# GpSimd's word additions and lower-half subtractions issued as two column halves, in an attention and MLP-mixer kernel

## The chip, the cores and the metric

The kernel runs on one core of one Trainium2 chip. The metric is the device time of one execution in microseconds (us). Five engines work side by side, each on its own queue of instructions in the order in which the program emitted them: TensorE (PE; its weight loads are shown as PEld), VectorE (DVE), ScalarE (ACT), GpSimd (POOL) and SyncE (SP), which here issues all transfers. They wait for each other by semaphores.

## The reference

A linear attention over four batches, four heads, 1088 positions and 32 channels per head; then two mixers, over positions and over channels:

```python
a = einsum('rd,bhsd->bhsr', S1, x); b = einsum('rd,bhsd->bhsr', S2, x)      # r = 8
phi(x) = (a_i * b_j), 64 features
kv = phi(k)^T v;  z = sum of phi(k) over positions
x = (phi(q) kv) / (phi(q) z + 1e-6)          # to [4, 1088, 128]
h = relu(x^T w_tok1) w_tok2                  # 1088 -> 256 -> 1088
u = x + h^T
out = u + relu(u w_ch1) w_ch2                # 128 -> 1536 -> 128
```

All inputs and the output are float32. The weights reach the kernel as float64 words (a 64-bit integer view), and the device itself turns them into float32.

## The kernel before, in words

The work goes batch by batch. For each batch there are `keys` (K: project, square into features, sum against v), queries (Q), `mixing` (A: attention, then the product with w_tok1, a transposition, the product with w_tok2), and for 384-column spans of all batches `channel_mix` (U: 12 hidden chunks; per chunk a first product with w_ch1 on PE, a ReLU copy on ACT, its remainder on DVE, a second product with w_ch2 on PE). From batch 1 on the mixing, and everywhere the channel mix, keeps float32 accuracy with three products of a short format: each operand is a high half (`halves[..][:, 0]`) and a low half (`halves[..][:, 1]`), and the products are high x high, low x high, high x low. Batch 0's mixing uses the undivided weights (`whole`).

The weights come in 17 pieces: `w00` to `w04` of w_tok1 (four of 512 columns, one, `w04`, of 256), `w10` to `w15` of w_tok2 (four of 384, two of 320), `w20` to `w22` of w_ch1 and `w30` to `w32` of w_ch2 (512 each). Each piece goes through this chain (`convert`, lines 333 to 372, then `divide_weight`, lines 437 to 451):

- `.abs` (ACT, line 343) and `.low` (ACT, line 347): the magnitude of the upper word, and the scaled lower word.
- `.clamp` (DVE, line 350), `.shift` (DVE, line 354, into PSUM bank `ps_h`), `.merge` (DVE, line 357).
- `.add` (POOL, lines 361 and 363): the lower word is added; this gives the float32 weight.
- `.hi` (ACT, line 444): the copy to the short format, the high half.
- `.lo` (POOL or DVE, whichever the planner takes, line 447): the weight less its high half.

What sets the order is a planner in the kernel (`Plan.run`, lines 187 to 261). It is a list scheduler that runs while the program is built: each step has an estimated cost for each engine that may do it (`act`, `dve`, `either`, ...), a level (its longest remaining path, plus `BOOST`, plus an entry of `LEAD` in ns), and the buffers it takes. The planner walks its own clock, always takes a step that can start first, among those the one of highest level, and emits it at once. So costs and levels alone decide each engine's order, and also how many filler products (`fill`, line 319, into an unused bank, row L322 of the profile) are put where PE is expected to be idle. Steps marked `port=True` on DVE (`.clamp` among them) and all POOL steps are kept apart on the planner's clock by one shared variable, `port`. For `.lo`, DVE is charged 1300 ns (`PBIAS`) on top. `LEAD` has 62 entries.

A short-format product can't start before the `.lo` that it reads; `is_whole` and `is_split` (lines 433 and 451) hold the last step of a piece's `.add` and `.lo`, and the products of A (`.t`, line 794; `.w`, line 912) and U (`.f`, line 974; `.s`, line 978) name them.

Of the kernel before, what the change touches and what calls it, by code (L numbers as in the profile page):

```python
# [15 lines left out]
ALU = mybir.AluOpType  # L16
# [23 lines left out]
def _spans():  # L40
# [27 lines left out]
    "A0.u2": 900.0,  # L68
    "A0.ul00": 51100.0,
    "A0.w2": 9300.0,  # L70
    "A1.t0": -6100.0,
    "A1.x": 36300.0,
    "A2.n0": 110900.0,
    "A2.n2": 110000.0,
    "A2.uh05": -52300.0,
    "A2.w2": -16300.0,
    "A3.n0": 18000.0,
    "A3.us1": 38200.0,
    "K0.s18": 52100.0,
# [6 lines left out]
    "Q0.b01": 29200.0,  # L86
    "Q0.b11": -8100.0,
    "Q0.p0": 54300.0,
    "Q1.m10": -20100.0,
    "Q1.m11": -21200.0,  # L90
    "Q2.p": 10200.0,
    "U0.f": 780300.0,
    "U11.f": 1400.0,
    "U2.f": -4000.0,
    "U4.f": 1480700.0,
    "U7.f": -2900.0,
# [8 lines left out]
    "w04.lo": -148800.0,  # L105
    "w04.low": 12100.0,
    "w10.abs": 19800.0,
    "w11.abs": 27600.0,
# [38 lines left out]
def f32(ap):  # L147
    return ap.bitcast(F32)
# [119 lines left out]
def act_sb(n):  # L268
    return {"act": 100 + 0.834 * n}
# [10 lines left out]
def either(n):  # L280
    return {"dve": 69 + 1.042 * n, "pool": 141 + 2.15 * n}
# [3 lines left out]
def attn_mixer_kernel(ctx: ExitStack, tc: tile.TileContext, qT, kT, v1, s64, wt1, wt2, wc1, wc2, out):  # L285
    nc = tc.nc
    engines = {"dve": nc.vector, "pool": nc.gpsimd, "act": nc.scalar}
# [3 lines left out]
    pool = ctx.enter_context(tc.tile_pool(name="pool", bufs=1))  # L291
# [32 lines left out]
    def load(name, dst, src, nbytes, after=(), takes=(), uses=(), boost=0.0):  # L324
# [3 lines left out]
        op.bytes, op.rate = nbytes, 395.0  # L328
        return op

    def convert(name, raw, n, loaded, dst=None, keep=None):


        t = {}
        c_hold, tail_hold, ps_hold = keep or Hold("c"), Hold("tail"), Hold("ps_h")
        words = raw.bitcast(I32).rearrange("p (n t) -> p n t", t=2)
        low, high = words[:, :, 0], words[:, :, 1]

        def magnitude(_):
            t["c"] = const.tile([P, n], I32, name="s_c") if keep else new("c", [P, CONV], I32)[:, :n]
            nc.scalar.activation(f32(t["c"]), f32(high), AF.Abs)  # L343

        def rest(_):
            t["tail"] = new("tail", [P, CONV], I32)[:, :n]
            nc.scalar.activation(t["tail"], low.bitcast(U32), AF.Copy, scale=2.0 ** -29)  # L347

        def clamp(_):
            nc.vector.tensor_scalar(f32(t["c"]), f32(t["c"]), LEAST, MOST, op0=ALU.max, op1=ALU.min)  # L350

        def shift(_):
            t["ps"] = bank("ps_h").bitcast(I32)[:, :n]
            nc.vector.tensor_scalar(t["ps"], t["c"], 3, 0x3FFFFFFF, op0=ALU.logical_shift_left, op1=ALU.bitwise_and)  # L354

        def merge(_):
            nc.vector.scalar_tensor_tensor(t["c"], high, -(1 << 30), t["ps"], op0=ALU.bitwise_and, op1=ALU.bitwise_or)  # L357

        def add(e):
            if dst:  # L360
                engines[e].tensor_tensor(dst(), t["c"], t["tail"], op=ALU.add)  # L361
            else:
                engines[e].tensor_tensor(t["c"], t["c"], t["tail"], op=ALU.add)
# [73 lines left out]
    def divide_weight(w, i, after=()):  # L437
        n = pieces[w, i].shape[1]
        name = f"w{w}{i}"
        m, t, c_hold = converted[w, i]  # L440

        def high(e):
            halves[w, i] = const.tile([P, 2, n], F32R, name=f"halves{w}{i}", tag=f"weight{w}{i}")
            nc.scalar.copy(halves[w, i][:, 0], f32(whole[w, i] if w < 2 else t["c"]))

        def low(e):
            engines[e].tensor_tensor(halves[w, i][:, 1], f32(whole[w, i] if w < 2 else t["c"]), f32(halves[w, i][:, 0]), op=ALU.subtract)  # L447
# [262 lines left out]
    def mixing(b, kvz_done, qp_done, qp_hold, boost, free):  # L710
# [63 lines left out]
        for g in range(3):  # L774
            def first(_, g=g):
# [117 lines left out]
        for i, (c0, cn) in enumerate(CHUNKS):  # L893
# [3 lines left out]
            def second(_, i=i, c0=c0, cn=cn):  # L897
# [45 lines left out]
    def channel_mix(segs):  # L943

        o_holds, outs = {}, {}
        for i, e0, e1 in segs:
# [3 lines left out]
            for e in range(e0, e1):  # L950
# [20 lines left out]
                        nc.tensor.matmul(outs[i][:, :cn], lhsT=part(3, at[3][e][0], l, at[3][e][1] * P, P), rhs=r[:, :cn], start=(e == 0 and m == 0), stop=(e == NCH - 1 and m == 2))  # L971
# [6 lines left out]
                s = plan.add(n + ".s", {"pe": cost}, second, [m, is_split[3, at[3][e][0]]], [o_hold] if e == 0 else (), [hid] + ([o_hold] if e else []), 0.0, 0, 2 * cost, [chain["s"]])  # L978
                chain["s"] = s
                if e == NCH - 6:  # L980
                    first_out = s
            if e1 == NCH:
# [6 lines left out]
                def add(_, i=i, cn=cn):  # L989
                    nc.vector.tensor_tensor(outs["sb", i][:, :cn], outs["sb", i][:, :cn], outs[i][:, :cn], op=ALU.add)  # L990
# [87 lines left out]
```

## Time and profile before

| | |
|---|---|
| time, median of 3 runs | 224.47 us (223.86 to 225.18) |
| the profiled execution's own time | 224.15 us |
| its span, first to last instruction | 222.3 us (1.85 us lie around it) |
| PE busy | 215.3 us |
| DVE busy | 141.3 us |
| ACT busy | 118.4 us |
| POOL busy | 80.5 us |

A row of the timeline has the start, the duration, the engine, the line of the program, the operation, what it writes and reads with its size, and how many instructions follow each other (`x2`); in brackets stands the engine's idle time before it and who ended it. The duration of a row of several runs from the start of the first to the end of the last. The instructions of DVE and POOL overlap a little at their ends, so the distance from one start to the next is often shorter than the duration. A step's name (w03.clamp) follows from the order in which the planner emitted the steps of that engine; most can also be told by size and line.

### The profile page before, as it was taken

How to read it: one execution, taken by the hardware profiler on the slowest of the kernel's cores; microseconds unless marked ns; L12 is line 12 of the kernel's file. 1: busy time of each engine (PE TensorE's matmuls, PEld its weight loads, DVE VectorE, ACT ScalarE, POOL GpSimd, SP SyncE). 2: the span in 40 equal slices, each digit the busy share in tenths (PEclk: the TensorE clock that was granted, in tenths of full speed). 3: DMA queues.
4: the chain of work that ended last, by engine and by line, in shares of the span. 5: the costliest groups of instructions: out<-in, count | busy, mean ns of one | idle time of the engine just before them, and what ended most of it. 6: DMA issues, size and time to landing. Idle time of an engine off the chain costs nothing.

```text
span 222.3 us, 4915 instructions
## 1 busy us (share of the span) xinstructions
PE 215.3 (97%) x1904; PEld 203.4 (91%) x1904; DVE 141.3 (64%) x273; ACT 118.4 (53%) x284; POOL 80.5 (36%) x85
## 2 busy tenths in 40 slices
PE   7999799999999999999999999999999999999994
PEld 7787658989988999999999899999999999999993
DVE  1689997998868465755825355657445655656662
ACT  4398499987446144553524354445235554445551
POOL 2074676989999401660500410443102300000000
PEclk9999999999999999999999999999999999999999
DMA  6999972999302999500060248400340000100000
GB/s 196 408 405 410 408 316 58 207 169 192 149 3 74 260 233 195 200 28 0 33 208 12 61 110 172 184 0 3 125 125 0 8 30 0 37 3 35 0 32 24
DMA packets 11207, 28.42 MB, mean 128 GB/s; under 512 B 1456, under 2 KB 5552, under 8 KB 11184
## 3 DMA queue, kind: packets, MB, share of 16 engines
q1 hardware_dynamic: 11184, 28.11, 41.4%
q8 instruction: 15, 0.25, 0.5%
q14 instruction: 8, 0.07, 0.1%
HBM read 23.27 MB, written 4.83 MB: 126 GB/s over the span
## 4 chain that ended last, share of the span: by engine, by line
PE 83%; DVE 9%; DMA 4%; issue 1%; POOL 1%; ACT 0%; POOLq 0%
PE ps_o L971 30%; PE ps_h L958 30%; PE ps_a L788 4%; PE ps_a L908 4%; PE ps_a L726 4%; DMA v_sb<-v 4%; PE ps_o L322 3%; DVE c L357 2%; PE ps_a L521 2%; DVE ps_h L354 2%; PE ps_a L474 2%; DVE c L350 2%; DVE hl L965 1%; PE ps_a L608 1%; DVE k_p L504 1%
## 5 line engine op out<-in xcount | busy, mean ns | idle before, releaser
L965 DVE SCALAR_TENSOR_TENSOR hl<-ps_h,hh 128x384 fp32r<-128x384 f32 (+2 forms) x144 | 75.3, 533 | 57.7 <-ACT hh L962 51.9
L962 ACT ACTIVATE hh<-ps_h 128x384 fp32r<-128x384 f32 (+2 forms) x144 | 67.8, 477 | 60.0 <-PE ps_h L958 51.6
L958 PE MATMUL ps_h<-uh,halves 128*128 128x384 f32 (+2 forms) x288 | 89.0, 332 | 0.1
L971 PE MATMUL ps_o<-hh,halves 128*128 128x384 f32 (+2 forms) x288 | 71.6, 330 | 0.1
L958 PEld LDWEIGHTS ps_h<-uh,halves 128*128 128x128 f32 x288 | 53.4, 188 | 1.9 <-issue 0.9
L971 PEld LDWEIGHTS ps_o<-hh,halves 128*128 128x128 f32 x288 | 50.2, 188 | 0.9 <-POOL halves L447 0.6
L971 PE MATMUL ps_o<-hl,halves 128*128 128x384 f32 (+2 forms) x144 | 47.2, 328 | 0.0
L958 PE MATMUL ps_h<-ul,halves 128*128 128x384 f32 (+2 forms) x144 | 46.9, 326 | 0.0
L958 PEld LDWEIGHTS ps_h<-ul,halves 128*128 128x128 f32 x144 | 27.1, 188 | 0.1
L882 POOL TENSOR_TENSOR ul<-us,uh 128x64 fp32r<-128x64 f32 (+4 forms) x15 | 9.5, 657 | 48.6 <-ACT uh L879 48.6
L971 PEld LDWEIGHTS ps_o<-hl,halves 128*128 128x128 f32 x144 | 27.1, 188 | 0.0
L706 POOL TENSOR_TENSOR qp<-qp,br 128x544 f32<-128x544 f32 x12 | 16.3, 1376 | 9.8 <-DMA br<-rows 9.8
L754 POOL TENSOR_TENSOR xl<-x,xh 128x384 fp32r<-128x384 f32 x9 | 9.0, 1020 | 15.9 <-ACT den L734 15.1
L504 DVE TENSOR_TENSOR k_p<-ps_a,a_sb 128x1024 f32<-128x1024 f32 (+1 forms) x12 | 10.9, 950 | 5.5 <-ACT a_sb L484 5.5
L361 POOL TENSOR_TENSOR whole<-c,tail 128x512 int32<-128x512 int32 (+3 forms) x11 | 12.0, 1093 | 4.8 <-DVE c L357 4.0
L322 PE MATMUL ps_o<-ident 128*128 128x128 f32 x66 | 11.0, 326 | 1.4 <-POOL ident masks.py:199 1.4
L322 PEld LDWEIGHTS ps_o<-ident 128*128 128x128 f32 x66 | 10.2, 233 | 1.9 <-POOL ident masks.py:199 1.4
L447 POOL TENSOR_TENSOR halves<-whole,halves 128x512 fp32r<-128x512 f32 (+3 forms) x11 | 11.9, 1103 | 0.0
L343 ACT ACTIVATE c<-doubles 128x512 f32<-128x512 f32 (+3 forms) x17 | 10.6, 637 | 1.8 <-POOL whole L361 1.4
L350 DVE TENSOR_SCALAR c<-c 128x512 f32<-128x512 f32 (+3 forms) x17 | 11.3, 677 | 0.0
L347 ACT ACTIVATE tail<-doubles 128x512 int32<-128x512 uint32 (+3 forms) x17 | 10.4, 644 | 1.5 <-POOL whole L361 1.5
L726 PEld LDWEIGHTS ps_a<-kvz,qp 128*64 128x64 f32 x288 | 9.0, 137 | 1.8 <-issue 1.2
(76 smaller groups left out, 238.8 us busy)
## 6 DMA issues: line engine op xcount, KB each, us to landing
qp<-rows SPq DMA_DIRECT2D x6, 544.0 KB, 9.4
br<-rows SPq DMA_DIRECT2D x12, 272.0 KB
doubles<-wc SPq DMA_DIRECT2D x6, 512.0 KB
v_sb<-v SPq DMA_DIRECT2D x4, 594.0 KB, 13.0
k_sb<-kT SPq DMA_DIRECT2D x4, 576.0 KB, 10.2
q_sb<-qT SPq DMA_DIRECT2D x4, 544.0 KB, 9.9
doubles<-wt SPq DMA_DIRECT2D x4, 512.0 KB, 7.7
xm<-xb SPq DMA_DIRECT2D x3, 576.0 KB, 2.9
```

The lines of the kernel that those rows point to most:

```text
L322: nc.tensor.matmul(spare_ps[:, :P], lhsT=ident, rhs=ident, start=True, stop=True)
L343: nc.scalar.activation(f32(t["c"]), f32(high), AF.Abs)
L350: nc.vector.tensor_scalar(f32(t["c"]), f32(t["c"]), LEAST, MOST, op0=ALU.max, op1=ALU.min)
L361: engines[e].tensor_tensor(dst(), t["c"], t["tail"], op=ALU.add)
L447: engines[e].tensor_tensor(halves[w, i][:, 1], f32(whole[w, i] if w < 2 else t["c"]), f32(halves[w, i][:, 0]), op=ALU.subtract)
L504: engines["pool" if on_pool else "dve"].tensor_tensor(t["k_p"][:pn, t0 * H:t1 * H], a.unsqueeze(3).broadcast_to([pn, n, R, R]), t["sb", t0 ...
L706: engines[e].tensor_tensor(qp[:, p, cs], qp[:, p, cs], t["br"][:, p, cs], op=ALU.mult)
L726: nc.tensor.matmul(x_ps[c:c + 64, o:o + 2 * (D + 1)], lhsT=qp[:, p, s0 + c:s0 + c + 64], rhs=kvz_all[b % 2][:, p, :], start=True, stop=True,)
L958: nc.tensor.matmul(h_ps[:, :cn], lhsT=part(2, at[2][e][0], l, at[2][e][1] * P, P), rhs=r[:, :cn], start=(m == 0), stop=(m == 2))
L962: nc.scalar.activation(t["hh"][:, :cn], t["h"][:, :cn], AF.Relu)
L965: nc.vector.scalar_tensor_tensor(t["hl"][:, :cn], t["h"][:, :cn], 0.0, f32(t["hh"][:, :cn]), op0=ALU.max, op1=ALU.subtract)
L971: nc.tensor.matmul(outs[i][:, :cn], lhsT=part(3, at[3][e][0], l, at[3][e][1] * P, P), rhs=r[:, :cn], start=(e == 0 and m == 0), stop=(e == ...
```

## The change

`add` and `low` get a slice of columns, and `in_parts` makes two planner steps out of each, with half of the columns and their own cost: `.add0` and `.add1` for the 17 pieces (the small constant `s` keeps its one addition on DVE), `.lo0` and `.lo1` for each division. The two halves of one step have the same predecessors; what followed one step now follows both (`.hi` waits for both additions, the products wait for both subtractions). Operations, operands and results are the same; 34 instructions become 68.

Besides, `LEAD` is other: it has 112 entries. Those of the six steps that were split pass to their halves (two of these with other values), 45 steps have an entry that had none, six values are changed and one entry (`U2.f`) is gone. The diff shows the core of it.

```diff
-    "A1.t0": -6100.0,
-    "A1.x": 36300.0,
-    "A2.n0": 110900.0,
+    "A1.n0": 71100.0,
+    "A1.t0": -6600.0,
+    "A1.w2": -100.0,
+    "A1.x": 65800.0,
...
+    "K2.p": 274800.0,
...
+    "w00.add0": 15600.0,
     "w00.hi": -188600.0,
-    "w00.lo": -296700.0,
-    "w02.lo": -1516300.0,
-    "w03.lo": -12100.0,
-    "w03.merge": -5300.0,
+    "w00.lo0": -296700.0,
+    "w00.lo1": -296700.0,
+    "w01.lo0": -270400.0,
+    "w01.lo1": -346700.0,
+    "w02.hi": -570400.0,
+    "w02.lo0": -1516300.0,
+    "w02.lo1": -1516300.0,
+    "w02.shift": -109900.0,
...
+    "w03.merge": 12400.0,
...
+    "w04.shift": 94300.0,
...
+    "w14.abs": -252800.0,
...
+    "w30.low": -71100.0,
...
+    def in_parts(n, make):
+
+        half = (n + 1) // 2
+        return [make(i, slice(a, min(n, a + half))) for i, a in enumerate(range(0, n, half))]
...
-        def add(e):
-            if dst:
-                engines[e].tensor_tensor(dst(), t["c"], t["tail"], op=ALU.add)
-            else:
-                engines[e].tensor_tensor(t["c"], t["c"], t["tail"], op=ALU.add)
+        def add(e, cs=slice(0, n)):
+            if dst and "to" not in t:
+                t["to"] = dst()
+            engines[e].tensor_tensor(t.get("to", t["c"])[:, cs], t["c"][:, cs], t["tail"][:, cs], op=ALU.add)
...
-        ways = {"dve": 69 + 2.084 * n} if keep else {"pool": 141 + 2.15 * n}
-        m = plan.add(name + ".add", ways, add, [m, r], (), [c_hold, tail_hold], port=True)
+        if keep:
+            return plan.add(name + ".add", {"dve": 69 + 2.084 * n}, add, [m, r], (), [c_hold, tail_hold], port=True), t, c_hold
+
+        m = in_parts(n, lambda i, cs: plan.add(f"{name}.add{i}", {"pool": 141 + 2.15 * (cs.stop - cs.start)}, lambda e, cs=cs: add(e, cs), [m, r], (), [c_hold, tail_hold], port=True))
...
-        def low(e):
-            engines[e].tensor_tensor(halves[w, i][:, 1], f32(whole[w, i] if w < 2 else t["c"]), f32(halves[w, i][:, 0]), op=ALU.subtract)
+        def low(e, cs):
+            engines[e].tensor_tensor(halves[w, i][:, 1, cs], f32(whole[w, i] if w < 2 else t["c"])[:, cs], f32(halves[w, i][:, 0, cs]), op=ALU.subtract)
...
-        m = plan.add(name + ".hi", act_sb(n), high, [m], (), use, order=after)
-        is_split[w, i] = plan.add(name + ".lo", either(n), low, [m], (), use, port=True)
+        m = plan.add(name + ".hi", act_sb(n), high, m, (), use, order=after)
+        is_split[w, i] = in_parts(n, lambda k, cs: plan.add(f"{name}.lo{k}", either(cs.stop - cs.start), lambda e, cs=cs: low(e, cs), [m], (), use, port=True))
```

The four places that name `is_whole` and `is_split` take the lists in place of the single steps.

More of the change, by code (lines that the diff above doesn't have):

```diff
@@ L81 @@
     "K1.c0": 73400.0,
+    "K1.s": 136500.0,
+    "K2.c0": -27100.0,
+    "K2.c8": -48200.0,
+    "K2.p": 274800.0,
+    "K2.s": 57400.0,
+    "K2.v4": 151900.0,
+    "K2.v8": 2570300.0,
     "K3.p": 82600.0,
@@ L88 @@
     "Q0.p0": 54300.0,
+    "Q1.c0": -5100.0,
+    "Q1.m00": -20200.0,
     "Q1.m10": -20100.0,
@@ L92 @@
     "U0.f": 780300.0,
+    "U0.oh": 14700.0,
+    "U1.f": 2100.0,
+    "U10.f": 1500.0,
     "U11.f": 1400.0,
-    "U2.f": -4000.0,
+    "U3.f": 74000.0,
     "U4.f": 1480700.0,
-    "U7.f": -2900.0,
+    "U5.f": 535300.0,
+    "U6.f": 371600.0,
+    "U7.f": 40600.0,
+    "w00.add0": 15600.0,
     "w00.hi": -188600.0,
-    "w00.lo": -296700.0,
-    "w02.lo": -1516300.0,
-    "w03.lo": -12100.0,
-    "w03.merge": -5300.0,
+    "w00.lo0": -296700.0,
[6 more added lines that the diff above has]
+    "w02.shift": -109900.0,
+    "w03.hi": 2300.0,
+    "w03.lo0": -67100.0,
+    "w03.lo1": -12100.0,
+    "w03.merge": 12400.0,
     "w04.abs": 70300.0,
@@ L104 @@
     "w04.hi": 8600.0,
-    "w04.lo": -148800.0,
-    "w04.low": 12100.0,
+    "w04.lo0": -148800.0,
+    "w04.lo1": -148800.0,
+    "w04.low": 92400.0,
+    "w04.shift": 94300.0,
     "w10.abs": 19800.0,
+    "w10.hi": 55100.0,
     "w11.abs": 27600.0,
@@ L113 @@
     "w12.abs": -1200.0,
-    "w12.lo": 7000.0,
+    "w12.lo0": 7000.0,
+    "w12.lo1": 7000.0,
     "w12.low": 159700.0,
     "w13.clamp": -55300.0,
+    "w13.lo0": 9300.0,
+    "w13.lo1": -171700.0,
+    "w13.low": -11300.0,
+    "w14.abs": -252800.0,
     "w14.low": -113600.0,
     "w15.clamp": 34000.0,
+    "w15.lo1": -11700.0,
     "w15.low": -82500.0,
-    "w20.add": -18200.0,
+    "w15.shift": 107300.0,
+    "w20.add0": -18200.0,
+    "w20.add1": -18200.0,
+    "w20.clamp": -10300.0,
     "w20.low": 45700.0,
     "w21.abs": -10800.0,
+    "w21.hi": -385300.0,
+    "w21.low": -82000.0,
+    "w22.abs": 600.0,
+    "w22.add1": -7900.0,
     "w22.low": 6300.0,
     "w30.abs": -6400.0,
+    "w30.low": -71100.0,
     "w30.merge": 75500.0,
     "w31.abs": -10200.0,
+    "w31.lo1": -25300.0,
     "w32.low": -196200.0,
@@ L793, in mixing @@
             last = plan.add(
-                f"{n}.t{g}", {"pe": 9 * 120.0 if b else 3 * 430.0}, first, [split[g]] + [(is_split if b else is_whole)[w] for w in sorted(need)],
+                f"{n}.t{g}", {"pe": 9 * 120.0 if b else 3 * 430.0}, first, [split[g]] + [a for w in sorted(need) for a in (is_split if b else is_whole)[w]],
                 [h_hold] if g == 0 else (), [x_hold] + ([xs_hold] if b else []) + ([h_hold] if g else []), boost, order=[last],
@@ L973, in channel_mix @@
                 cost = 3 * cn * 0.453
-                f = plan.add(n + ".f", {"pe": cost}, first, u_done[i] + [is_split[2, at[2][e][0]]], [ps], [u_holds[i]], 0.0, 0, 2 * cost, [chain["f"]])
+                f = plan.add(n + ".f", {"pe": cost}, first, u_done[i] + is_split[2, at[2][e][0]], [ps], [u_holds[i]], 0.0, 0, 2 * cost, [chain["f"]])
                 chain["f"] = f
@@ L977, in channel_mix @@
                 m = plan.add(n + ".l", dve(cn), low, [m], (), [ps, hid])
-                s = plan.add(n + ".s", {"pe": cost}, second, [m, is_split[3, at[3][e][0]]], [o_hold] if e == 0 else (), [hid] + ([o_hold] if e else []), 0.0, 0, 2 * cost, [chain["s"]])
+                s = plan.add(n + ".s", {"pe": cost}, second, [m] + is_split[3, at[3][e][0]], [o_hold] if e == 0 else (), [hid] + ([o_hold] if e else []), 0.0, 0, 2 * cost, [chain["s"]])
                 chain["s"] = s
```

10 lines of the change are left out of this document (9 added, 1 removed).

## The prediction

> **What bounds the kernel now.** I read the page, then the busy times by stretch, then the timelines of PE, DVE and POOL over the first 75 us, then the chain of waits. On the page I look for the engine that is never free, and for the groups that the change touches:
>
> ```profile
> PE 215.3 (97%) x1904; PEld 203.4 (91%) x1904; DVE 141.3 (64%) x273; ACT 118.4 (53%) x284; POOL 80.5 (36%) x85
> L361 POOL TENSOR_TENSOR whole<-c,tail 128x512 int32<-128x512 int32 (+3 forms) x11 | 12.0, 1093 | 4.8 <-DVE c L357 4.0
> L447 POOL TENSOR_TENSOR halves<-whole,halves 128x512 fp32r<-128x512 f32 (+3 forms) x11 | 11.9, 1103 | 0.0
> ```
>
> PE is busy for 97% of the span, POOL for 36%, but the shares mix unlike stages. By stretch (busy time and count of PE, PEld, DVE, ACT, POOL, then clock, DMA share, GB/s):
>
> ```profile
> 20.00:30.00 10.00, 7.99 (x66) 6.62 (x65) 9.69 (x23) 5.90 (x14) 6.59 (x7) 1.00 1.03 410
> 30.00:40.00 10.00, 9.88 (x74) 7.28 (x74) 8.51 (x16) 9.67 (x21) 6.68 (x6) 1.00 0.46 151
> 40.00:50.00 10.00, 10.00 (x140) 9.28 (x137) 10.00 (x17) 9.05 (x25) 9.14 (x9) 1.00 0.94 175
> 50.00:60.00 10.00, 9.91 (x57) 9.60 (x57) 8.77 (x17) 6.30 (x14) 9.71 (x8) 1.00 0.78 190
> 60.00:70.00 10.00, 10.00 (x127) 8.47 (x125) 6.98 (x14) 5.04 (x15) 10.00 (x12) 1.00 0.06 21
> ```
>
> From 40 us on PE has no free time to give. Between 20 and 40 us DVE is the full engine (9.69 and 8.51 of 10); from 40 to 70 us POOL is (9.14, 9.71, 10.00). So a gain has to come out of PE's open time before about 38 us, and POOL has no room to pay for it between 40 and 70. PE's open time is waiting and filler (L322):
>
> ```profile
> 21.92 1.60 PE L322 MATMUL ps_o<-ident 128*128 128x128 f32 x12
> 25.16 2.86 PE L782 MATMUL ps_a<-whole,x 128*128 128x256 f32 x12 [1.64 <-DVE x L744]
> 30.85 1.28 PE L322 MATMUL ps_o<-ident 128*128 128x128 f32 x10
> 32.06 1.30 PE L663 MATMUL ps_a<-q_sb,s_rows 64*32 64x272 f32 x16
> 36.20 1.20 PE L971 MATMUL ps_o<-hh,halves 128*128 128x384 f32 x2
> 51.41 0.51 PE L958 MATMUL ps_h<-uh,halves 128*128 128x384 f32 x2
> ```
>
> From the first filler to the next real product these are 3.24 us (21.92 to 25.16) and 1.21 us (30.85 to 32.06). The two products at 36.20 last 1.20 us where two of that size last 0.51 (51.41), so 0.69 more. That makes 5.1 us, the ceiling of what this stretch can give.
>
> **Part 1: the clamps wait for a shorter neighbour.** DVE's clamp (L350) is the one DVE step of a weight that suffers beside POOL:
>
> ```profile
> L350 DVE TENSOR_SCALAR c<-c x17: 288/428/1524, 9.7 to 57.3; 128x512 f32<-128x512 f32 x10, 128x384 f32<-128x384 f32 x4, 128x320 f32<-128x320 f32 x2, 128x256 f32<-128x256 f32 x1
> 18.15 1.52 DVE L350 TENSOR_SCALAR c<-c 128x512 f32<-128x512 f32 x1
> 18.12 1.28 POOL L361 TENSOR_TENSOR whole<-c,tail 128x512 int32<-128x512 int32 x1 [1.05 <-DVE c L357]
> 22.37 0.88 DVE L350 TENSOR_SCALAR c<-c 128x384 f32<-128x384 f32 x1
> 22.27 0.77 POOL L361 TENSOR_TENSOR whole<-c,tail 128x256 int32<-128x256 int32 x1 [1.13 <-DVE c L357]
> 29.95 1.15 DVE L350 TENSOR_SCALAR c<-c 128x512 f32<-128x512 f32 x1
> 29.76 1.05 POOL L361 TENSOR_TENSOR whole<-c,tail 128x384 int32<-128x384 int32 x1
> 30.78 1.45 POOL L447 TENSOR_TENSOR halves<-c,halves 128x512 fp32r<-128x512 f32 x1
> 38.88 0.42 DVE L350 TENSOR_SCALAR c<-c 128x512 f32<-128x512 f32 x1
> L882 POOL TENSOR_TENSOR ul<-us,uh 128x128 fp32r<-128x128 f32 x2 | 0.9, 462 | 14.5 <-ACT uh L879 14.5
> ```
>
> A clamp of 512 columns takes 0.42 us alone (38.88). w03's at 18.15 began 0.03 us after w02's addition on POOL (18.12 to 19.40) and ended at 19.67, 0.27 after it: it stood until the POOL instruction had ended. The trace also shows who goes next. At 29.95 w30's clamp stood through w12's addition (to 30.81) and ended at 31.10; w20's subtraction, the next on POOL, started by its row at 30.78 and took 1.45 us, where the one at 35.62 (below) takes 1.28. DVE slips in between two POOL instructions that follow each other at once. So a halved addition frees the clamp after its first half:
>
> - At 18.15 the half (256 columns, 0.77 by the row at 22.27) is over 0.51 us sooner than the 1.28.
> - At 22.37 the half has 128 columns (0.46 by L882) in place of 256 (0.77): 0.31.
> - At 29.95 the half has 192 columns, between 0.46 and 0.77, estimated 0.62, in place of 1.05: 0.43.
>
> These 1.25 us lie on the path. The first two stand on DVE's full queue ahead of the division A0.d1 (L742, L744) for which PE waits at 25.16; the third stands ahead of w30's merge, which starts the piece that PE's stall at 36.20 needs. [...]
>
> **Part 2: each half pays its fixed part again.**
>
> ```profile
> 68.00 0.76 POOL L447 TENSOR_TENSOR halves<-whole,halves 128x256 fp32r<-128x256 f32 x1
> 68.69 2.98 POOL L754 TENSOR_TENSOR xl<-x,xh 128x384 fp32r<-128x384 f32 x3
> 71.62 2.55 POOL L447 TENSOR_TENSOR halves<-whole,halves 128x512 fp32r<-128x512 f32 x2
> 74.11 0.89 POOL L987 TENSOR_TENSOR o_sb<-uh,ul 128x320 f32<-128x320 f32 x1
> 33.41 1.29 POOL L363 TENSOR_TENSOR c<-c,tail 128x512 int32<-128x512 int32 x1 [1.18 <-DVE c L357]
> 34.65 1.00 POOL L361 TENSOR_TENSOR whole<-c,tail 128x384 int32<-128x384 int32 x1
> 35.62 1.28 POOL L447 TENSOR_TENSOR halves<-c,halves 128x512 fp32r<-128x512 f32 x1
> ```
>
> From start to start a subtraction of 256 columns costs 0.69 us (68.00 to 68.69), one of 512 costs 2.49 / 2 = 1.245 (71.62 to 74.11): two halves cost 0.14 more. By durations it is 2 x 0.76 - 1.28 = 0.24. I take 0.14, since queued halves overlap like these, and 0.2 as the other end. 34 splits make 4.8 to 6.8 us of POOL. It counts where POOL is on the path: w30's addition (33.41), w13's behind it (34.65), then w30's subtraction (35.62 to 36.90), for which PE stands at 36.20. Three splits put this 0.14 + 0.2 + 0.14 = 0.48 us later (the middle one with two halves of 0.62 against 1.0 to 1.05). [...]
>
> In the additions before that, POOL waits for DVE's merges anyway (1.18 us at 33.41), which covers the extra; without that cover each follower would be 0.14 later. ACT's `.hi` waits for two additions in place of one; behind it in ACT's queue stand the ReLU copies, and PE's second products wait for those. Both additions come from one queue, so only the later counts, priced above; the same holds for the products' wait for two subtractions. If the planner gave a half to DVE, DVE would have some 0.4 us more and POOL 0.69 less; I count nothing for it. The split moves no transfer.
>
> **Part 3: one later wait.** The last place where DVE leads PE in the chain of waits:
>
> ```profile
> 50.21 0.70 DVE c L357
> 50.95 1.31 PE ps_h L958 x6
> 50.53 0.86 PE L958 MATMUL ps_h<-uh,halves 128*128 128x384 f32 x2
> 45.75 1.24 DVE L350 TENSOR_SCALAR c<-c 128x512 f32<-128x512 f32 x1
> ```
>
> w32's merge holds the bank that PE wants to write: two products last 0.86 us in place of 0.51. w32's clamp ahead of it lost 1.24 - 0.42 = 0.82 us to a subtraction of 384 columns; 0.43, as at 29.95, is saved and covers the 0.35.
>
> **Part 4: the new levels.** The trace of before can't show an order that wasn't run. At best the new `LEAD` closes what is left of the 5.1 us (4 us), at worst it puts a POOL backlog in front of PE (first rival). The levels of w04.shift and w03.merge rise, which works for A0.t2; that of w02.shift falls, which works against A0.t1; both products stand at 25.16. I take zero, between the signs.
>
> **Sum.** 224.15 us (the profiled execution) - 1.25 + 0.48 - 0.35 = 223.0 us. That execution is 0.32 us under the median of the runs, 224.47, and 0.5% (1.1 us) is about what a measurement of this kernel can tell from no change: against the median the forecast is faster by 1.4 us, just past that. Its own range is 222.5 (the 0.48 hidden) to 223.8 (half of the 1.25 and 0.2 for each split).
>
> **Rivals.** *POOL becomes the bound (slower).* In the stretch that ends with w00's subtraction (71.62 to 72.91), which A1.t0 on PE reads:
>
> ```profile
> 41.74:72.91 31.17, 31.08 (x333) 28.32 (x332) 26.66 (x48) 20.65 (x54) 30.06 (x28) 1.00 0.57 129
> 73.68 0.40 PE L788 MATMUL ps_a<-halves,xh 128*128 128x256 f32 x2
> ```
>
> 18 of its POOL instructions are split (the additions of w31, w22, w32, w15, w14; the subtractions of all pieces but w20, w30, w01, w02), which costs 2.5 to 3.6 us; POOL's idle time there is 31.17 - 30.06 = 1.1, and the products start 0.8 after w00's subtraction. If order and room stay, PE waits 0.6 to 1.7 us. With the 0.48 of part 2 and no saving on DVE that reaches PE: 224.15 + 0.48 + 1.15 = 225.8 us (225.2 to 226.4). It decides once a split costs over 0.11 us. Against it: the planner counts 141 ns for each extra instruction, the 0.14 of the rows, and can put U2's products ahead of A1.t0.
>
> *The time won on DVE turns into other waits (no change).* ACT is as full as DVE from 30 to 40 us (9.67 of 10); if its copies are late next, PE keeps its stalls: 224.2 to 224.6 us.
>
> *The new order closes more (faster).* If half of the 4 us left goes, beside the 1.1: 221.0 us (220.5 to 222.4). For it: 3.24 us of it are one stall behind one DVE step, A0.d1, and its place in DVE's queue is a matter of levels.
>
> *The change doesn't do what it says (no change).* If both halves run before a waiting clamp, nothing is saved: 224.15 + 0.48 = 224.6 us. The rows at 29.95 and 30.78 speak against it.
>
> **How the numbers follow.** Forecast 0.38 (0.24 faster by over 0.5%, 0.14 within), closer order 0.24 (all faster), other waits 0.17 (within), halves without a gap 0.06 (0.04 within, 0.02 slower), POOL backlog 0.15 (0.13 slower, 0.02 within): faster 0.48, same 0.37, slower 0.15. The range leaves out the far ends of the two outer cases: 220.8 to 225.6 us.
>
> **What would show it.** Right: clamps beside POOL of at most 1.0 us; 68 instructions in L361, L363 and L447's groups, of 0.76 us at 256 columns, and POOL busy for 5 to 7 us more; the first product of A0.t1 before 24.6 us; the stall at 36.20 shorter or earlier. Wrong: clamps as long as before; PE waiting for POOL's halves near 73 us; PE's stretch after 75 us no longer gapless, for which the forecast has no term.

## The result and the profile after

The changed kernel takes 225.79 us (median of 20 runs), the kernel before in the same job 224.22 us (20 runs): ratio 1.0066, 95% interval 1.0049 to 1.0083. It is slower by 0.66%, 1.5 us; the forecast was 223.0, and the range, 220.8 to 225.6, ends 0.2 us short of it. Two of the changed kernel's 20 runs took 266 and 303 us at a granted clock of 0.76 and 0.66, which the ratio leaves out, and one of the two was the profiled run, so the lines below are those of a later execution at full clock (225.21 us, span 223.4).

From its page, the busy times (engine, share, instructions):

```profile
PE 215.9 (97%) x1918; PEld 204.3 (91%) x1918; DVE 139.1 (62%) x273; ACT 117.9 (53%) x284; POOL 85.8 (38%) x119
```

Its halves of 256 columns among the groups by form (busy us, mean ns, idle before them):

```profile
L503 POOL TENSOR_TENSOR halves<-c,halves 128x256 fp32r<-128x256 f32 x12 | 9.2, 783 | 0.1
L417 POOL TENSOR_TENSOR c<-c,tail 128x256 int32<-128x256 int32 x12 | 9.1, 772 | 1.4 <-DVE c L412 0.6 <-DMA br<-rows 0.5 <-ACT tail L402 0.2
```

And its clamps by their line (shortest, median and longest in ns):

```profile
L405 DVE TENSOR_SCALAR c<-c x17: 306/419/952, 9.3 to 51.4; 128x512 f32<-128x512 f32 x10, 128x384 f32<-128x384 f32 x4, 128x320 f32<-128x320 f32 x2, 128x256 f32<-128x256 f32 x1
```

So far as foretold: 34 instructions more on POOL (119 against 85) and 5.3 us more of its time (85.8 against 80.5), halves of 256 columns near 0.76 us, and no clamp above 0.95 us where one had taken 1.52. By stretch (busy PE, PEld, DVE, ACT, POOL, clock, DMA share, GB/s):

```profile
20.00:30.00 10.00, 9.09 (x72) 7.23 (x71) 9.62 (x21) 5.91 (x13) 8.12 (x13) 1.00 1.03 408
...
40.00:50.00 10.00, 8.98 (x114) 7.99 (x110) 9.63 (x18) 8.69 (x23) 9.57 (x15) 1.00 0.89 186
50.00:60.00 10.00, 10.00 (x78) 9.36 (x78) 6.61 (x15) 6.33 (x14) 6.78 (x11) 1.00 0.78 199
60.00:70.00 10.00, 9.26 (x151) 8.59 (x148) 6.46 (x13) 3.82 (x13) 10.00 (x15) 1.00 0.29 96
```

Two stretches in which PE had been full, 40 to 50 and 60 to 70, are so no longer (8.98 and 9.26, both 10.00 before), and POOL, 9.71 from 50 to 60 before, stands idle for 3.2 us there. PE's timeline names the places:

```profile
21.87 1.38 PE L372 MATMUL ps_o<-ident 128*128 128x128 f32 x10
23.72 2.86 PE L838 MATMUL ps_a<-whole,x 128*128 128x256 f32 x12 [0.47 <-DVE x L800]
29.41 1.72 PE L372 MATMUL ps_o<-ident 128*128 128x128 f32 x14
31.06 0.69 PE L719 MATMUL ps_a<-q_sb,s_rows 64*32 64x272 f32 x16
32.83 0.83 PE L372 MATMUL ps_o<-ident 128*128 128x128 f32 x6
35.50 0.60 PE L1027 MATMUL ps_o<-hh,halves 128*128 128x384 f32 x2
...
48.53 0.45 PE L1014 MATMUL ps_h<-uh,halves 128*128 128x384 f32 x1 [0.81 <-DVE hl L1021]
...
69.10 2.32 PE L577 MATMUL ps_a<-v_sb,k_p 128*64 128x66 f32 x72 [0.74 <-issue]
```

The stall ahead of A0.t1 went from 3.24 us to 1.85 (21.87 to 23.72), and the two products that had lasted 1.20 us at 36.20 last 0.60 at 35.50. But from A0.t1 to Q1's product it is 7.34 us in place of 6.90 (25.16 to 32.06 before), and six filler products stand at 32.83. Then come two waits that weren't there, at 48.53 and 69.10. To sum such places I take, for each two neighbouring products on PE, the distance of their starts beyond the median distance that products of that shape on those tiles have in the kernel before, and count filler whole; the rest is the same 196.4 us in every kernel. So the differences of the last column are those of PE's whole time, while the split by stretch depends on the medians taken, by some tenths of a us. PE's open time in us:

| kernel | 20 to 40 us | 40 to 70 us | whole span |
|---|---|---|---|
| before | 8.30 | 2.25 | 21.13 |
| changed | 7.92 | 3.45 | 22.28 |
| split in the old order | 7.85 | 4.89 | 24.01 |
| three additions split, old order | 7.33 | 2.01 | 19.92 |
| changed, rows sooner | 8.15 | 2.63 | 21.50 |
| changed, rows sooner, `U0.ol` later | 7.93 | 2.51 | 21.13 |

The change gained 0.38 us in the lead-in and lost 1.20 us from 40 to 70, and 0.42 more from 70 to 80, where PE is never idle. Of the other engines' rows, in order of time, the first five belong to the wait at 48.53, the others to that at 69.10:

```profile
45.72 1.44 DVE L405 TENSOR_SCALAR c<-c 128x320 f32<-128x320 f32 x2 [0.34 <-ACT c L398]
45.88 0.96 ACT L1018 ACTIVATE hh<-ps_h 128x384 fp32r<-128x384 f32 x2
46.05 0.81 POOL L417 TENSOR_TENSOR c<-c,tail 128x256 int32<-128x256 int32 x1
47.08 0.48 DVE L409 TENSOR_SCALAR ps_h<-c 128x320 int32<-128x320 int32 x1
47.47 1.01 DVE L1021 SCALAR_TENSOR_TENSOR hl<-ps_h,hh 128x384 fp32r<-128x384 f32 x2
...
58.11 1.37 POOL L762 TENSOR_TENSOR qp<-qp,br 128x544 f32<-128x544 f32 x1 [3.08 <-PE ps_o L1027]
...
66.60 1.97 POOL L1043 TENSOR_TENSOR o_sb<-uh,ul 128x384 f32<-128x384 f32 x2
67.64 0.56 DVE L1046 TENSOR_TENSOR o_sb<-o_sb,ps_o 128x384 f32<-128x384 f32 x1 [2.56 <-POOL o_sb L1043]
68.44 0.56 DVE L800 TENSOR_TENSOR x<-ps_a,rec 128x384 f32<-128x384 f32 x1
```

First: DVE had two clamps (w15, w32) and a shift ahead of the remainders `U0.l`, and w32's clamp stood through a POOL addition (46.05 to 46.86). ACT's `hh` were ready at 46.84, `U0.l` began at 47.47, and PE waited for it. Second: POOL waited 3.08 us for data at 58.11 (the profile names a PE product that had long ended; in the run below in which Q1's rows are issued sooner it doesn't wait). It came to `U0.oh` only at 66.60, DVE's `U0.ol` stood 2.56 us for that, A1's divisions stood behind `U0.ol` on DVE, and PE went on at 69.10, just after the division at 68.44 had read its bank to the end (69.00); that this bank is what K2's products need is read from these times, and the runs below that take `U0.ol` out of the way agree.

Q1's row transfers, as the kernel before and then the changed one issue them (SP's queue; `x4` are the writes, the rows below them the last two reads):

```profile
34.14 1.76 SPq L680 DMA_DIRECT2D rows<-abT  x4
40.08 1.20 SPq L696 DMA_DIRECT2D br<-rows  x2
```

```profile
34.92 3.21 SPq L736 DMA_DIRECT2D rows<-abT  x4
42.32 1.20 SPq L752 DMA_DIRECT2D br<-rows  x2
```

The last reads were issued 2.24 us later although Q1's product ended 1.6 us sooner (31.75, 33.36 before): the new order puts Q1's two copies on ACT behind steps of the weights (they start at 33.32 and 34.48, 1.6 and 2.7 us after the product's end; before, the first starts right behind it, at 33.43).

### The profile page after: what moved, and what is told of

The parts are those of the page before. It is cut to its first block, busy times and chain, and to the rows that moved or that the text cites. A ratio compares the mean times of both kernels' runs of the same rounds, so it can differ in the third digit from the quotient of the medians.

```text
span 264.4 us, 5035 instructions
## 1 busy us (share of the span) xinstructions
PE 259.3 (98%) x1918; PEld 234.5 (89%) x1918; DVE 141.6 (54%) x273; ACT 119.2 (45%) x284; POOL 85.3 (32%) x119
## 4 chain that ended last, share of the span: by engine, by line
PE 94%; DMA 2%; DVE 2%; POOL 1%; issue 0%; SPq 0%; ACT 0%; DVEq 0%; POOLq 0%; ACTq 0%
PE ps_h L1014 33%; PE ps_o L1027 33%; PE ps_a L844 4%; PE ps_a L782 4%; PE ps_a L964 4%; PE ps_a L577 3%; PE ps_o L372 3%; PE ps_a L530 2%; DMA k_sb<-kT 2%; PE ps_a L960 2%; PE ps_a L664 1%; PE ps_o L577 1%; PE ps_h L664 1%; PE ps_a L719 1%; PE ps_a L838 1%; POOL c L417 1%
## 5 line engine op out<-in xcount | busy, mean ns | idle before, releaser
L1014 PE MATMUL ps_h<-uh,halves 128*128 128x384 f32 (+2 forms) x288 | 101.7, 377 | 0.0
L1027 PE MATMUL ps_o<-hh,halves 128*128 128x384 f32 (+2 forms) x288 | 83.4, 378 | 0.0
L1014 PEld LDWEIGHTS ps_h<-uh,halves 128*128 128x128 f32 x288 | 57.3, 200 | 4.7 <-ACT tail L402 0.5
L1027 PEld LDWEIGHTS ps_o<-hh,halves 128*128 128x128 f32 x288 | 55.6, 201 | 3.7 <-issue 0.2
L1027 PE MATMUL ps_o<-hl,halves 128*128 128x384 f32 (+2 forms) x144 | 54.0, 375 | 0.0
L1014 PE MATMUL ps_h<-ul,halves 128*128 128x384 f32 (+2 forms) x144 | 53.7, 373 | 0.0
L417 POOL TENSOR_TENSOR whole<-c,tail 128x256 int32<-128x256 int32 (+3 forms) x22 | 13.7, 644 | 2.7 <-ACT tail L402 1.3
L503 POOL TENSOR_TENSOR halves<-whole,halves 128x192 fp32r<-128x192 f32 (+3 forms) x22 | 13.3, 627 | 0.8 <-ACT halves L500 0.7
L844 PE MATMUL ps_a<-halves,xh 128*128 128x256 f32 x54 | 11.6, 307 | 0.0
L782 PE MATMUL ps_a<-kvz,qp 128*64 128x66 f32 x288 | 11.6, 246 | 0.0
```

The source lines that it names most:

```text
L417: engines[e].tensor_tensor(t.get("to", t["c"])[:, cs], t["c"][:, cs], t["tail"][:, cs], op=ALU.add)
L503: engines[e].tensor_tensor(halves[w, i][:, 1, cs], f32(whole[w, i] if w < 2 else t["c"])[:, cs], f32(halves[w, i][:, 0, cs]), op=ALU.subtract)
L782: nc.tensor.matmul(x_ps[c:c + 64, o:o + 2 * (D + 1)], lhsT=qp[:, p, s0 + c:s0 + c + 64], rhs=kvz_all[b % 2][:, p, :], start=True, stop=True,)
L844: nc.tensor.matmul(t["h_ps"][:, :DTOK], lhsT=t[l][:m, i, :], rhs=part(0, piece, r, j * DTOK, DTOK)[:m], start=(i == 0 and k == 0), stop=(i ...
L1014: nc.tensor.matmul(h_ps[:, :cn], lhsT=part(2, at[2][e][0], l, at[2][e][1] * P, P), rhs=r[:, :cn], start=(m == 0), stop=(m == 2))
```

## The experiments

My theory after this reading was that the halves do what was foretold, that the order under the new `LEAD` loses more than they gain, and that its two waits can be removed. The rival: the 34 additional instructions cost the time, whatever the order. Ratios are to the kernel before on the same chip. "Port" in the expectations is the planner's variable, used for what a clamp from SBUF to SBUF waits for beside POOL; the runs show how long such clamps stand (2.72 us in the old order with halves), not what lies behind it.

**Split or order.** First the changed kernel again.

> The changed kernel again, for a profile at full clock. It was measured at 1.0066 times the time of before. Theory A (the order that the new levels make is worse on the chip than the old one; the halves are harmless): PE's open time is at new places, waits for ACT or POOL that the order of before did not have, and the clamps are as short as forecast (at most 1.0 us). Theory B (the halves cost more than they save): PE waits for POOL's halves, and POOL is full from 40 to 75 us with 5 to 7 us more busy time. Both expect 1.005 to 1.009.

225.97 us, 1.0065 [1.0035, 1.0094]: the result repeats. The later execution that gave the profile above:

> The changed kernel once more, for a profile at full clock. Theory N1 (its new order has a longer lead-in): 80 fillers instead of 66, 14 of them after 15 us, so PE starts its gapless stretch 1.3 to 2.0 us later than before, and from 45 us on PE has no wait of over 0.6 us. Theory N2 (as in the old order with halves, a clamp loses the port late): a clamp of over 1.5 us after 40 us, PE idle for over 1 us behind it, and a granted clock of under 0.8 for some us after that.

Neither holds as it stands: there are 80 fillers, but A0.t1 comes 1.4 us sooner, two waits of 0.81 and 0.74 us stand after 45 us, and no clamp takes over 0.95. Next the order of before, with each of the 34 steps issued as two instructions in its old place (the same loop in `low`):

```diff
...
-                engines[e].tensor_tensor(t["c"], t["c"], t["tail"], op=ALU.add)
+            to = dst() if dst else t["c"]
+            for cs in [slice(0, n)] if keep else [slice(0, n // 2), slice(n // 2, n)]:
+                engines[e].tensor_tensor(to[:, cs], t["c"][:, cs], t["tail"][:, cs], op=ALU.add)
```

> The order of before, untouched: each addition and subtraction of a weight is merely issued as two instructions in a row in its old place. Theory A: the clamps beside POOL fall to about 0.9 us, and the time is 0.993 to 1.002 times that of before (the forecast of 223.0 belongs to this kernel rather than to the change). Theory B: 18 splits between 41.7 and 72.9 us push the weights for A1.t0 back, PE waits there, 1.004 to 1.010.

228.62 us, 1.0180 [1.0144, 1.0217], far worse than the changed kernel and outside both theories. So the split itself can cost more than the new order does. Its lead-in is as foretold (w03's and w04's clamps together 1.18 us instead of 1.73). These rows, the chain from w30's addition to its subtraction and the two products that wait for w32's merge, are taken up again below:

```profile
32.60 1.44 POOL L362 TENSOR_TENSOR c<-c,tail 128x256 int32<-128x256 int32 x2 [0.49 <-DVE c L357]
35.09 1.43 POOL L447 TENSOR_TENSOR halves<-c,halves 128x256 fp32r<-128x256 f32 x2
49.81 0.86 PE L958 MATMUL ps_h<-uh,halves 128*128 128x384 f32 x2
```

What it loses stands at 54 to 61 us, in the timeline:

```profile
52.25 2.84 POOL L447 TENSOR_TENSOR halves<-c,halves 128x256 fp32r<-128x256 f32 x4
53.84 2.72 DVE L350 TENSOR_SCALAR c<-c 128x320 f32<-128x320 f32 x1
55.05 1.33 POOL L706 TENSOR_TENSOR qp<-qp,br 128x544 f32<-128x544 f32 x1
57.08 0.45 PE L958 MATMUL ps_h<-uh,halves 128*128 128x384 f32 x1 [1.78 <-DVE hl L965]
```

The two stretches behind PE's wait (columns as above):

```profile
57.10:61.20 4.10, 4.10 (x15) 4.10 (x16) 3.32 (x8) 0.49 (x1) 3.13 (x4) 0.62 0.29 118
61.20:65.00 3.80, 3.80 (x21) 3.54 (x20) 1.68 (x3) 2.17 (x5) 3.80 (x7) 0.96 0.00 0
```

w15's clamp began during the first half of w32's subtraction and stood through that half, the second half and Q1's multiplication, which ended at 56.38: 2.72 us, where the same clamp takes 1.17 in the kernel before (53.89) and ended behind one subtraction. A remainder for PE stands behind it on DVE; PE waited 1.78 us, and for 4.1 us thereafter the granted clock was 0.62 in the mean (0.96 in the next 3.8): from 58.06 to 61.25 products of 384 columns start 0.32 us apart, 0.17 before the wait.

The changed kernel's code with the levels of before:

```diff
-    "A1.t0": -6600.0,
+    "A1.t0": -6100.0,
...
-    "w02.shift": -109900.0,
```

> The changed code with the old level table, each entry of a split step given to both halves; the planner orders anew with its own costs. Theory A: near before, 0.995 to 1.003, since the loss belongs to the new table. Theory B: 1.004 to 1.010, since the halves are there.

229.13 us, 1.0181 [1.0142, 1.0219], again outside both, with PE waits of 1.35 us before 39.33 and 2.65 us before 134.32 (the product ahead of it ends at 131.67). And the reverse, before's code with the new levels:

```diff
-    "A1.t0": -6100.0,
+    "A1.t0": -6600.0,
...
+    "w02.shift": -109900.0,
```

> The code of before (whole additions and subtractions) with the new level table, the entries of two halves joined (the higher value, or zero where only one half had an entry and that is negative). Theory A: the loss is here as well, 1.003 to 1.015. Theory B: no loss, 0.995 to 1.002.

243.28 us, 1.0824 [1.0782, 1.0866], with one wait of 9.54 us before 110.79. A table of levels is good only for the steps that it was set for. The order of the changed kernel can be had without its halves, by emitting a whole instruction at the first half's place and nothing at the second's (the same in `add`):

```diff
         def low(e, cs):
+            if cs.start:
+                return
+            cs = slice(0, n)
```

> The changed kernel's order with whole instructions: the first half's place takes the whole addition or subtraction, the second half's place nothing. N1: the lead-in is a matter of the order, the time stays 1.003 to 1.015 times that of before. If the halves themselves are the loss (their fixed part on the path), it falls to 0.996 to 1.002.

226.08 us, 1.0104 [1.0084, 1.0124], against 1.0066 with halves. Within the new order the halves gain some 0.4%; that order, with whole instructions at these places, loses about 1%, 2.3 us. In the old order it is the halves that lose, in the new one the order.

**Which halves, and why.** The old order with two of the 34 whole again, w22's and w32's subtractions:

```diff
-            for cs in (slice(0, n // 2), slice(n // 2, n)):
+            for cs in [slice(0, n)] if (w, i) in ((2, 2), (3, 2)) else [slice(0, n // 2), slice(n // 2, n)]:
```

> The old order with all halves in place, but the subtractions of w22 and w32, between which w15's clamp stood for 2.7 us, left whole. Theory P (the loss of the halves in the old order is this one clamp, which lost the port to three POOL instructions in a row, with PE idle and its clock down after it): the loss of 1.018 goes, 0.995 to 1.004. Theory B (the halves' fixed parts): 1.012 to 1.018 stays.

224.87 us, 1.0049 [1.0022, 1.0075]: these two account for 1.3 of the 1.8%. With the 17 additions in halves and every subtraction whole:

> The old order with all 17 additions issued as halves, the subtractions whole. Theory P (w15's clamp loses the port only behind the halved subtractions of w22 and w32): no late loss, 0.995 to 1.002. If the halved additions themselves let clamps starve or their fixed part decides, 1.004 or more.

223.89 us, 0.9991 [0.9976, 1.0006], no change, though the three additions of part 1 are among the 17. To see whether POOL's work is what holds w15's clamp, the kernel with all 34 steps split, with this one clamp writing into the PSUM bank that its shift fills anyway:

```diff
+            if name == "w15":
+                t["ps"] = bank("ps_h").bitcast(I32)[:, :n]
+                nc.vector.tensor_scalar(f32(t["ps"]), f32(t["c"]), LEAST, MOST, op0=ALU.max, op1=ALU.min)
+                return
...
```

> Before's order with all 34 steps as two halves (228.62 us), but w15's clamp writes into a PSUM bank, and its shift works there, so that this one DVE instruction no longer goes from SBUF to SBUF. Theory (shared port): the clamp takes 0.3 to 0.6 us in place of 2.72, PE's wait of 1.78 us and the granted clock of 0.62 behind it are gone, and the time falls by about 3 us, to 225 to 226.2 us, near the run with w22's and w32's subtractions whole (224.87). Rival (the clamp is held by its data, or by the DVE queue): it still ends after POOL's third instruction, and the time stays at 228 to 229 us.

224.18 us, 1.0008 [0.9991, 1.0025]. One instruction out of GpSimd's way takes back the 1.8% (PE still waits 0.90 us here):

```profile
54.15 0.49 DVE L352 TENSOR_SCALAR ps_h<-c 128x320 f32<-128x320 f32 x1
55.16 0.45 PE L965 MATMUL ps_h<-uh,halves 128*128 128x384 f32 x1 [0.90 <-DVE hl L972]
```

Lastly, only w32's subtraction whole (`(w, i) == (3, 2)`), which leaves whole instructions from the clamp's start on:

> Before's order with all steps halved but w32's subtraction, which is one instruction again. Theory (the clamp loses the port to every POOL instruction that is already queued when the one ahead of it ends): it stands now through the whole w32.lo and, if Q1's multiplication is queued right behind, through that too, 1.2 to 2.6 us: 224.9 to 227 us, by whether Q1's rows have come. Rival (only several short instructions in a row keep a clamp waiting): the clamp takes 1.2 us, as in the kernel before, and the time is 224.5 to 225.3 us.

The twelve runs fall apart, five from 224.9 to 225.8 us and seven from 226.6 to 229.4; ratio 1.0095 [1.0059, 1.0131] without the four longest, 1.015 by the medians of all (227.36 and 223.99). The mean granted clock is 0.998 to 1.000 in the five and 0.985 to 0.991 in six of the seven. The profile is of one that lost:

```profile
53.92 3.87 DVE L350 TENSOR_SCALAR c<-c 128x320 f32<-128x320 f32 x1
58.30 0.69 PE L958 MATMUL ps_h<-uh,halves 128*128 128x384 f32 x1 [2.94 <-DVE hl L965]
```

This clamp stood through three instructions of about 1.3 us each, two of which began when it was already waiting (POOL was busy without a gap from 53 to 57 us), so short ones aren't needed for it. In the kernel before, the clamp also began during a whole w32.lo, and was served right behind it (53.89 to 55.06; the subtraction ends at 54.88). That the short runs are those in which the clamp was served sooner is read from the times and clocks; no trace shows one of them. If so, who comes next, the clamp or POOL's next instruction, isn't settled by the order of the queues. What does settle it stays open.

Then the three additions that part 1 names and nothing else (w02, w04, w12), in the old order:

```diff
+            for cs in [slice(0, n // 2), slice(n // 2, n)] if name in ("w02", "w04", "w12") else [slice(0, n)]:
```

> The old order; only the three additions of the prediction's part 1 (w02, w04, w12) are issued as halves. The prediction's step gives 1.25 us less with 0.2 more for w12: 0.994 to 0.998 if the saving reaches the end, 0.998 to 1.002 if it is lost on the way.

223.22 us, 0.9968 [0.9947, 0.9988]; the profiled run of it was 224.22 us and caught late rows of Q1:

```profile
56.69 1.37 POOL L705 TENSOR_TENSOR qp<-qp,br 128x544 f32<-128x544 f32 x1 [2.23 <-DMA br<-rows]
...
61.06 1.34 PE L903 MATMUL ps_a<-whole,hTl 128*128 128x320 f32 x4 [1.73 <-POOL whole L362]
```

Again, on another chip:

> The kernel before with the additions of w02, w04 and w12 alone in halves, again, beside the run with the three clamps in PSUM, on the same chip: 222.9 to 223.5 us, ratio 0.995 to 0.999, as before; a ratio of 1 or more would say that its first result was a matter of the chip.

222.93 us, 0.9935 [0.9912, 0.9958]: faster than both kernels. Pairs of clamps on DVE (w04 with w03, w10 with w11, w13 with w30) and PE's first stall, in the kernel before and then in this run:

```profile
17.95 1.73 DVE L350 TENSOR_SCALAR c<-c 128x256 f32<-128x256 f32 x2
22.10 1.15 DVE L350 TENSOR_SCALAR c<-c 128x384 f32<-128x384 f32 x2
29.60 1.50 DVE L350 TENSOR_SCALAR c<-c 128x384 f32<-128x384 f32 x2
```

```profile
18.07 1.18 DVE L350 TENSOR_SCALAR c<-c 128x256 f32<-128x256 f32 x2
21.67 0.88 DVE L350 TENSOR_SCALAR c<-c 128x384 f32<-128x384 f32 x2
22.07 1.60 PE L322 MATMUL ps_o<-ident 128*128 128x128 f32 x12
24.47 2.86 PE L781 MATMUL ps_a<-whole,x 128*128 128x256 f32 x12 [0.79 <-DVE x L743]
28.93 1.09 DVE L350 TENSOR_SCALAR c<-c 128x384 f32<-128x384 f32 x2
```

The pairs are shorter by 0.55, 0.27 and 0.41 us, 1.23 in all, and the stall by 0.84 (2.40 for 3.24); the span is 1.2 us shorter (221.1). The same three clamps out of POOL's way with nothing halved, by the PSUM edit above for w03, w11 and w30:

> The kernel before, nothing halved and in its own order; the clamps of w03, w11 and w30 write into the PSUM bank that their shift writes anyway, and the shift works there. Theory (the waits on the shared port lie on the path): these clamps take 0.5 to 0.7 us whatever POOL does, in place of 1.53, 0.88 and 1.15; A0.t1 on PE starts 1.1 to 1.3 us sooner, and the time falls by 0.8 to 1.5 us, to 222.5 to 223.2 us, below the run with three halved additions. Rival (the gain goes into a wait further on, on ACT or in the bank that is now taken sooner): PE's first product of A0.t1 comes sooner, but its open time from 20 to 40 us falls by less than 0.5 us, and the time stays at 223.6 to 224.2 us.

223.94 us, 0.9978 [0.9961, 0.9994]: a gain, but a small one.

```profile
17.67 0.69 DVE L352 TENSOR_SCALAR ps_h<-c 128x512 f32<-128x512 f32 x1
19.25 0.43 DVE L361 TENSOR_SCALAR ps_h<-c 128x256 int32<-128x256 int32 x1 [0.89 <-ACT xT L637]
...
56.55 1.36 POOL L713 TENSOR_TENSOR qp<-qp,br 128x544 f32<-128x544 f32 x1 [1.38 <-DMA br<-rows]
...
60.96 1.34 PE L911 MATMUL ps_a<-whole,hTl 128*128 128x320 f32 x4 [0.92 <-POOL whole L368]
```

w03's clamp takes 0.69 us, but it holds a bank for longer, and the next shift waits 0.89 us for one that ACT has to free. The lead-in gains as much as with three halves all the same: the pair of clamps that DVE starts at 45.04 in the kernel before starts at 43.97 in both runs, 1.07 us sooner. This execution loses it again behind that: POOL waits 1.38 us for Q1's rows, and PE 0.92 us behind POOL. In the second run with three halves POOL didn't wait there (two multiplications of Q1 from 53.74 to 56.65), while in the first, of the same program, it waited 2.23 us (before 56.69). So the wait for these rows can differ from one execution to another, and this run doesn't tell what the longer hold on the bank costs.

**Which wait of the new order.** Single steps of the changed kernel, moved in the order of emission and nothing else. `U0.ol` (and its output) later, so that A1's divisions come first:

```diff
+MOVES = [("U0.ol", "A1.d2"), ("U0.out", "A1.d2")]   # emit the first just ahead of the second
```

> The changed kernel with one step moved on DVE's queue: U0.ol, which stands there for 2.56 us waiting for POOL's U0.oh, comes behind A1.d0 and A1.d1 and the next U1.l instead of ahead of them (its store behind it). Theory Q (the changed kernel's loss is two waits of PE of about 1 us each, at 47.5 and at 68.0 us; the second is this one): the PE wait at 68 us goes, 0.7 to 1.0 us less, 1.001 to 1.004 times before. If the wait at 68 us has another cause, 1.006 stays.

225.23 us, 1.0051 [1.0031, 1.0071]. The wait at 69 us is gone (PE's open time from 60 to 70 falls from 1.31 to 0.54 us); the gain by the ratios is 0.15%, within the intervals. w32's clamp behind the two `U0.l` (`("w32.clamp", "w32.shift")`):

> The changed kernel with w32's clamp behind the two U0.l instead of ahead of them; the clamp stood for 0.95 us beside POOL's halves, and PE waited 1.0 us at 47.5 for the second U0.l. Theory Q: this wait falls to under 0.4 us, 1.001 to 1.004 times before, unless w32, later by some 0.6 us, is awaited instead (then 1.004 to 1.008).

225.66 us, 1.0073 [1.0049, 1.0098]. The wait at 48.53 is gone, but w32's merge is now late for a bank: PE waits 0.48 us before 50.09, and 0.44 us before 69.68. Both moves:

> Both moves at once. Theory Q: the loss is gone, 0.996 to 1.000 times before. Otherwise 1.003 or more.

225.49 us, 1.0067 [1.0041, 1.0092]: the loss isn't gone. Waits of 0.46 us (before 49.52, for a merge) and 0.66 us (before 60.04, for a transfer) stand in their place. Then the cause of POOL's late start, Q1's copies on ACT, right behind their product:

```diff
+MOVES = [("Q1.c0", "w21.low"), ("Q1.c1", "w21.low")]
```

> The changed kernel with ACT's two copies Q1.c0 and Q1.c1 emitted right behind the product that they read, ahead of w21's and w30's steps. Theory (late rows): the reads of Q1's rows are issued 1 to 2 us sooner, POOL's first multiplication of Q1 waits 1 to 2 us in place of 3.08, U0.oh and U0.ol end sooner, and PE's wait of 0.9 us at 68 us is gone: 224.8 to 225.2 us, ratio 1.002 to 1.006. Rival (the reads' arrival has little to do with their issue, or POOL is late for its own work): the multiplication waits as long as before and the time stays at 225.5 to 226.1 us. ACT's w21.abs, w21.low and w30.hi come up to 0.7 us later; if one of them is needed at once, a new wait of PE shows between 34 and 50 us.

224.58 us, 1.0019 [1.0004, 1.0035]: 0.47% better than the changed kernel, 1.05 us. SP's first read (39.62 in the changed kernel), POOL's multiplication and DVE's `U0.ol`:

```profile
35.90 0.63 SPq L760 DMA_DIRECT2D qp<-rows  x1
55.15 1.35 POOL L773 TENSOR_TENSOR qp<-qp,br 128x544 f32<-128x544 f32 x1
65.17 0.55 DVE L1057 TENSOR_TENSOR o_sb<-o_sb,ps_o 128x384 f32<-128x384 f32 x1
```

No wait is left on POOL, nor on `U0.ol`. In all five profiles of the new order whose last reads were issued after 41 us, POOL waits 2.3 to 4.0 us for Q1's rows; here and in the next run, with the last reads before 39 us, it doesn't. With that and `U0.ol` later:

> As the run before, and U0.ol with the output behind it emitted after A1.d1, as in the earlier run that moved U0.ol alone (225.23 us). Theory (late rows): with the rows sooner there is no wait at 68 us left for U0.ol to cause, so this equals the run before within 0.3 us. Rival (DVE's order alone matters): it equals the earlier run with U0.ol moved alone, and lies 0.5 us under the run before.

224.06 us, 1.0009 [0.9992, 1.0026]. The step from the run before is too small for these intervals to tell apart from none; with both moves the changed kernel is level with the one before.

## Why the prediction was wrong, step by step

- **Part 1, -1.25 us: right where it was measured alone.** Three halved additions in the old order shorten the three pairs of clamps by 0.55, 0.27 and 0.41 (0.51, 0.31 and 0.43 foretold), 1.23 us, and the span by 1.2. The waits lie on the path, as assumed.
- **"DVE slips in between two POOL instructions that follow each other at once": failed as a rule.** It rested on one clamp at 29.95. w15's clamp lost to the next instruction twice over in two kernels (2.72 and 3.87 us), and the kernel with one whole subtraction goes either way from run to run. Written into PSUM, the same clamp took 0.49 us for 2.72 with POOL as busy; who is next when it goes from SBUF to SBUF no run shows. In the changed kernel this cost nothing (no clamp over 0.95 us). In the old order it cost 1.8%, and the rival of halves that run before a waiting clamp had it at 0.06, at a price of no change.
- **Part 2, +0.48 us: right in the old order.** POOL's total is 5.3 us for 34 splits, 0.16 each (0.14 to 0.2 foretold). On the path, from w30's addition to the end of its subtraction, all halves in the old order take 3.92 us (32.60 to 36.52) where the kernel before takes 3.49 (33.41 to 36.90), 0.43 more. Parts 1 and 2 together can be read at the two products that wait for w32's merge: they start at 50.53 before, at 49.81 with all halves in the old order, 0.72 us sooner (0.77 foretold), and at 49.46 with three halved additions, 1.07 sooner (1.05 foretold, with 0.2 for w12). In the changed kernel the term can't be told from the order; the products at 36.20 stand for less there.
- **Part 3, -0.35 us: didn't come.** In the old order with all halves, w32's two products for that bank still last 0.86 us (49.81): PE comes there sooner by as much as the merge.
- **Part 4, new levels at zero: the step that failed for this kernel.** The order that the new levels make costs some 2.3 us with whole instructions (1.0104), where the sum had nothing for it; the halves take 0.4% of that back. In the profile the new order cuts the first stall to 1.85 us (3.24 before, 2.40 with three halves in the old order), gives 1.0 of these 1.39 us back before 40 us (0.38 is left), and then makes two new waits; from 40 to 80 us it loses 1.6. That is the "order" rival with the opposite sign. The traces of before couldn't show it, but the only bound on this side was POOL's backlog: three levels of steps ahead of A0 were weighed, and Q1's copies, U0's remainders and `U0.ol` weren't, though `Q1.c0` and `U0.oh` have entries in the new `LEAD` that they had not before.
- **The signs.** All four signs of being right came (clamps, POOL's groups, A0.t1 before 24.6, the stall at 36.20), none of those of being wrong did, and the kernel is slower: they test parts 1 and 2, and none of them tests the order behind 40 us.
- **The POOL rival named 225.8 us**, and that is the time, by luck. Its mechanism wasn't there: POOL was idle for 3.2 us between 50 and 60, no product waited for its halves near 73 us, and most of the time came back with two copies on ACT. POOL was late because its data were.

Of the changed kernel's loss of 1.5 us, 1.05 went when the rows were read sooner (by the two intervals, roughly 0.5 to 1.6). About 0.2 more went with `U0.ol` moved as well, within the error; PE's open time is then that of before (21.13 us in both). The wait at 48.53 is named by the trace alone: the move that removes it brings others, so its price stays open. That the old order loses more under 34 splits than the new one (1.0180 and 1.0066) is the one clamp that stood for 2.72 us: with it written into PSUM the old order is at 1.0008. Why that, and 17 halved additions (0.9991), gain less than three (0.9968 and 0.9935) is shown in part only, by part 2's chain: 0.43 us longer with all halves, 0.28 with the additions alone.

## What to carry to other kernels

Split the instruction that stands in front of a waiting neighbour, and only that one: three splits gained 0.3 to 0.65%, all 34 lost 0.7 to 1.8%. A clamp's wait beside POOL can also be removed at the waiting instruction: one clamp into PSUM took back 1.8% in the old order, while three such clamps gained 0.2%, in an execution with late rows. When a change brings a new order with it, follow each transfer's issue and each step that moved past another before counting the order at zero, and name a sign that tests the order too.

## What the runs showed of the hardware

- A DVE clamp from SBUF to SBUF stood for 3.87 us through three GpSimd instructions of about 1.3 us, two of which began when it was already waiting; the same program's runs fell into 224.9 to 225.8 and 226.6 to 229.4 us.
- PE's wait of 1.78 us (57.08, all halves in the old order) was followed by 4.1 us at a granted clock of 0.62, so that by an estimate it cost 4.1 x 0.38 = 1.6 us beyond its own length, and one of 2.94 us (58.30, only w32's subtraction whole) by 0.66 from 57 to 62 us; the waits of 0.81 and 0.74 us in the changed kernel left it at 1.00. So did the wait of 2.65 us with the levels of before (134.32; the mean clock of that execution is 1.000), so in these runs the length of a wait alone doesn't decide it. What does, no run shows.
- A clamp of 320 columns into PSUM took 0.49 us (54.15) with GpSimd busy throughout (52.37 to 55.18); one of that size from SBUF to SBUF, begun while GpSimd was idle, took 0.32 (58.78 with all halves in the old order, GpSimd idle for 0.96 us before 58.95).
- Q1's rows kept GpSimd waiting for 2.23 us in one execution of the kernel with three halved additions (56.69) and not at all in an execution of the same program on another chip (53.74 to 56.65).
